# Copies of h and its maxima issued by SyncE instead of GpSimd, and two of the four products of the ones moved behind a later transform

## The chip, the cores and the metric

The kernel runs on one core of a Trainium2 chip. The time is that of the device, in microseconds, from a run of the whole program. Before the change it is 1114.31 us, the median of 3 runs (1113.95 to 1114.52). One further execution was profiled; its own time is 1113.99 us, and the span of the trace is 1112.2 us.

## The reference

```python
# x: (8, 3136, 256)
X = np.fft.fft(x, axis=1)
X = np.fft.fft(X, axis=2)
x = X.real.reshape(25088, 256)          # 8 * 3136 tokens
h = x @ w_in                            # (25088, 1024)
e = np.exp(h - h.max(-1))
sm = e / (e.sum(-1) + 1e-09)
solu = h * sm
mu, var = mean(solu), mean((solu - mu) ** 2)
ln = (solu - mu) / np.sqrt(var + 1e-06) * g_ln
out = ln @ w_out                        # (25088, 256)
```

A two-dimensional Fourier transform whose real part goes, token by token, through a first weight, a softmax-weighted linear unit, a layer norm, and a second weight. All of it is float32.

## The kernel before, in words

**Units.** The transform over 3136 positions is split as 49 x 64. The kernel treats the eight sequences as four pairs, and for each pair it goes over 24 frequencies k1 of the 49; a unit is one pair at one frequency. Since the input is real, a frequency and its mirror give the same even part and opposite odd parts, so each unit has 128 rows of even part and odd part and two "signs", s = 0 and s = 1, of h: the sum and the difference of the two. That makes 96 units, and two more are put in at places 90 and 91 (`order_of`): the units of frequency zero, each holding the 32 columns of four sequences (`t.m` is 0 or 1 for these two and None for all others). 98 units in all, and 49 batches of two.

**Steps.** After an opening, a loop over i goes through the units. In step i the program works on several of them at once, each engine's instructions in program order (the order is written out by hand and the tiles' dependencies supply the semaphores):

- unit i: `even` (line 318, VectorE), `up` (line 305, TensorE, the first weight), `join` for both signs (lines 334 and 338, VectorE: h and, by the same instruction, its negated maximum), `expo` for both signs (line 346, ScalarE), `product` for both signs (line 353, VectorE), `square` for both signs (line 360, ScalarE), and `turn_both` (line 425, VectorE).
- unit i + 2: `second_transform` (line 269, TensorE), whose result q is taken by ScalarE (`take2`, line 275); then `spread` (line 280), a small copy issued by SyncE.
- unit i - 5: `Down`, the second weight by seven block products instead of eight: p1, p4, p5, p6, p2, p3, p7 (line 502, TensorE, each eight matmuls in the trace). p5, p6, p3 and p7 use sums of blocks, S. X, onto which p6 accumulates, is seeded by a copy of ScalarE (`seed`, line 528) of what p1 made. In ScalarE's queue that copy stands behind the squares of unit i - 1 and the take of q.
- unit i - 4: `sums` (line 495, four additions on GpSimd) make its S. The first of them is made to wait for VectorE's last product of unit i - 1.
- the batch of units i - 2 and i - 1, when i is even: `move_blocks` (line 462), 16 DMAs issued by SyncE, the rest of the transposition.
- unit i - 6: `store`. The rows of sign 0 of a batch go out by four DMAs of SyncE (line 600) when its second unit is done; those of sign 1 by an indirect DMA of GpSimd (line 589).

**SyncE's order in a step.** Stores of unit i - 6 (odd i only, once the batches are shared), spread of unit i + 2, and further down, for even i, the moves. A DMA's waits are made by the engine that issues it, at its place in that engine's program.

**Frequency 1568.** One frequency of the 3136, half of them, comes out of no unit's rows by itself. Its eight rows of h, one for each sequence, are computed apart (`Half`), over the steps before unit 90: `half.h` holds the rows and `half.row` the negated maxima. In steps 90 and 91 (the units of frequency zero) four of them each are put into rows 0, 32, 64 and 96 of sign 1 of h, and their maxima into `nmax`. `give` (lines 876 to 879) does that, after the unit's join and before its exponentials, by two DMAs of GpSimd: line 878 copies the four rows of 1024 numbers, line 879 the four maxima. For these two units the join makes s = 1 first (line 334, then the negation, line 322), then s = 0 (line 338). The second exponential needs both copies.

In GpSimd's queue, step i has: mirror sums (not in steps 90 and 91), `sums`, `give`, `power` (line 415), `store` of sign 1.

**The opening.** The weights come as float64 and are narrowed on the chip. The second weight Wo is narrowed in four pieces of two chunks (`narrow_out`, line 677, VectorE, with ScalarE making the exponents by lines 651 to 655). Its mean over the 1024 rows, wbar, is later subtracted from it (`centre`). The mean's sum is made by TensorE as products with a matrix of ones (`mean_out`, line 782), in two parts: first the four chunks 0 to 3 of Wo, in the opening, ahead of the transforms of units 0 and 1 (line 269); then, in step 1, two chunks that GpSimd's `fold_out` has made of chunks 4 to 7. `keep_mean` (line 786, ScalarE) takes the result. `begin(1)`, near the end of step 0, holds `up` of unit 1 and the transform of unit 3. In step 1 `turn_whole` (line 443) transposes unit 0 on TensorE, ahead of the second part of the mean.

Of the kernel before, what the change touches and what calls it, by code (L numbers as in the profile page):

```python
# [17 lines left out]
P = 128  # L18
# [5 lines left out]
NH = N2 // 2  # L24
# [31 lines left out]
def kernel(  # L56
# [19 lines left out]
    nc = tc.nc  # L76
    B, S, D = x.shape
    FF = moe_w_in.shape[1]
    KF = FF // P
# [26 lines left out]
    Wo = const.tile([P, KF, D], FP32, name="Wo")  # L106
    Ws = const.tile([P, 4, KF // 2, P], FP32, name="Ws")
    ones_ident = const.tile([P, 2 * P], FP32, name="ones_ident")
    ones, ident = ones_ident[:, 0:P], ones_ident[:, P:]
# [11 lines left out]
    def result(i):  # L121

        return banks[i % 4]
# [168 lines left out]
    def column(t):  # L292

        ps = result(3)[:, 0:1]
        nc.tensor.matmul(ps, t.q[0:1, P : 2 * P], ones[0:1, 0:1], start=True, stop=True)
        t.r = small.tile([P, 1], FP32, tag="r", name="r")
        nc.vector.tensor_copy(out=t.r, in_=ps)

    def up(t, c):

        ps = ps_h.tile([P, FF], FP32, tag=f"h{c}", name=f"ps_h{c}")
        whole_even = c == 0 and t.at in MIDDLE
        for half in range(2):
            fs = slice(half * HW, (half + 1) * HW)
            nc.tensor.matmul(ps[:, fs], t.q[:, c * P : (c + 1) * P], Wi[:, c, fs], start=True, stop=not whole_even)  # L305
        if whole_even:
            for half in range(2):
                fs = slice(half * HW, (half + 1) * HW)
                nc.tensor.matmul(ps[:, fs], t.q[0:1, P : 2 * P], w_mid[0:1, fs], start=False, stop=True)
        return ps  # L310

    def even(t, ps):

        t.ev = fpool.tile([P, FF], FP32, tag="ev", name="ev", bufs=1)
        if t.at in MIDDLE:
            nc.scalar.copy(t.ev, ps)
            return
        nc.vector.scalar_tensor_tensor(out=t.ev, in0=w_mid, scalar=t.r, in1=ps,  # L318
                                       op0=ALU.mult, op1=ALU.add)
# [8 lines left out]
    def join(t, s):  # L328

        if t.nmax is None:  # L330
            t.nmax = small.tile([P, 2], FP32, tag="nmax", name="nmax")
        t.h[s] = fpool.tile([P, FF], FP32, tag="h", name="h", bufs=2)
        if s and t.m is not None:
            nc.vector.tensor_tensor_reduce(out=t.h[s], in0=t.ev, in1=t.odd, scale=0.5, scalar=-3.0e38,
                                           op0=ALU.subtract, op1=ALU.max, accum_out=t.nmax[:, s : s + 1])
            negate(t.nmax[:, s : s + 1])
            return
        nc.vector.tensor_tensor_reduce(out=t.h[s], in0=t.h[0] if s else t.ev, in1=t.odd, scale=1.0 if s else -0.5,  # L338
                                       scalar=3.0e38, op0=ALU.add, op1=ALU.min, accum_out=t.nmax[:, s : s + 1])
# [16 lines left out]
    def square(t, s):  # L356

        if s == 0:
            t.ssq = small.tile([P, 2], FP32, tag="ssq", name="ssq")
        nc.scalar.activation(out=t.h[s], in_=t.u[s], func=ACT.Square, bias=t.usum[:, s : s + 1], scale=-float(FF),  # L360
                             accum_out=t.ssq[:, s : s + 1])
# [70 lines left out]
    def turn_whole(t, late=False):  # L432

        uT = t.batch.uT[:, t.w].rearrange("p c i (n s) -> p c (i n) s", s=2)
        n = KF // 2
        t.wait = []
        for s in t.signs:
            for half in range(2):
                bank = (1, 2, 0, 1)[2 * s + half] if late else 2 * s + half + 1
                ps = result(bank).rearrange("p (c k) -> p c k", c=n)  # L440
                for c in range(n):
                    f = half * n + c
                    nc.tensor.matmul(ps[:, c, :], t.u[s][:, f * P : (f + 1) * P], ident, is_transpose=True,
                                     start=(c == 0), stop=(c == n - 1), skip_group_check=True)
                if s or late and half:
                    t.wait.insert(0 if bank == 0 else len(t.wait), (uT[:, half * n : (half + 1) * n, :, s], ps))
                else:
                    nc.scalar.copy(uT[:, half * n : (half + 1) * n, :, s], ps)
# [231 lines left out]
    class Weights:  # L680
# [91 lines left out]
            n = KF // 4 * D  # L772
            nc.gpsimd.tensor_tensor(out=self.part, in0=w[:, 0:n], in1=w[:, n:], op=ALU.add)

        def mean_out(self, half):
            if half == 0:
                self.cs = result(3)[:, 0:D]
                parts = [Wo[:, c, :] for c in range(KF // 2)]
            else:
                parts = [self.part[:, c * D : (c + 1) * D] for c in range(KF // 4)]  # L780
            for c, i in enumerate(parts):
                nc.tensor.matmul(self.cs, ones, i, start=half == 0 and c == 0, stop=half == 1 and c == KF // 4 - 1,
                                 skip_group_check=True)

        def keep_mean(self):
# [56 lines left out]
    class Half:  # L842
# [32 lines left out]

        def give(self, t):
            of = slice(4 * t.m, 4 * t.m + 4)
            nc.gpsimd.dma_start(out=t.h[1][0 : P : NH], in_=self.h[of])
            nc.gpsimd.dma_start(out=t.nmax[0 : P : NH, 1:2], in_=self.row[of, 1:2])

    with tc.manual_schedule():
        pairs = [Pair(p) for p in range(NP)]
        first, weights = pairs[0], Weights()
# [107 lines left out]
        def second_transform(i):  # L991
            if i < len(units):
                t = units[i]
                if t.m is None:
                    take2(t, transform2(pairs[t.p], t.k))
                else:
                    t.q = q_self[t.m]
                if i not in (2, 3) + MIDDLE:
                    spread(t)

        def enter(i):
            cur = units[i]
            if i % 2 == 0:
                batches.append(Batch(i // 2))
            cur.batch, cur.w = batches[-1], i % 2

        def begin(i):

            cur = units[i]
            enter(i)  # L1010
            ps = up(cur, 0)
            if i in (2, 3):
                cur.odd = up(cur, 1)
                column(cur)
            even(cur, ps)
            if i not in (2, 3):
                cur.odd = up(cur, 1)
            second_transform(i + 2)
# [8 lines left out]
        for i in range(whole + 1):  # L1027
            cur = units[i]
            prv = units[i - 1] if i else None
            if prv:  # L1030
                turn_whole(prv, i == 1)
                if i == 1:
                    square(prv, 1)
            if i == 1:
                weights.mean_out(1)
            for s in cur.signs:
                join(cur, s)
            if i == 0:
                weights.narrow_out(3, (2,))
                weights.fold_out()  # L1040
            if 1 < i < whole:
                for o, ps in prv.wait:
                    nc.vector.tensor_copy(out=o, in_=ps)
            for s in cur.signs:
                expo(cur, s)
            if i == 1:
                weights.keep_mean()
            if i in (1, whole):
                for o, ps in prv.wait:
                    nc.scalar.copy(o, ps)  # L1050
            if i == 0:
                begin(1)
            done = units[0 if i == 2 else i - 1 : i] if i > 1 else []
            for t in done:
                stats(t)
            if i == whole:
                nxt = units[i + 1]
                enter(i + 1)
                even(nxt, up(nxt, 0))
            if i == whole:  # L1060
                other_pairs(i, ahead, "fold")
            for s in cur.signs:
                product(cur, s)
                if i < whole and s == 0:
                    square(cur, s)
            if i == 1:
                weights.centre(cur)
            if i == 2:
                weight_sums(cur)
            if i < whole:  # L1070

                if i:
                    begin(i + 1)
                if i:
                    square(cur, 1)
            else:
                for s in cur.signs:
                    square(cur, s)
                other_pairs(i, ahead, "mirror", cur)
                sums(units[1], None, part=slice(2, 4))  # L1080
                turn_both(cur)
                stats(cur)
            for work in ("mirror", "fold", "load") if i < whole else ("load",):
                other_pairs(i, ahead, work, cur)
            if i == whole - 1:
                sums(units[1], None, part=slice(0, 2))
            for t in done:
                power(t)
# [9 lines left out]
        for i in range(whole + 1, len(units) + lag + 1):  # L1098
# [30 lines left out]
            if cur:  # L1129
# [3 lines left out]
                if i == SELF_STEPS[-1]:  # L1133
                    half = Half()
# [165 lines left out]
```

## Time and profile before

| | |
|---|---|
| median of 3 runs | 1114.31 us |
| lowest, highest | 1113.95, 1114.52 us |
| the profiled execution's own time | 1113.99 us |
| its span | 1112.2 us |
| TensorE matmul busy | 1094.5 us, 98% of the span |
| TensorE weight load | 876.8 us, 79% |
| VectorE | 971.2 us, 87% |
| ScalarE | 801.3 us, 72% |
| GpSimd | 786.6 us, 71% |

How to read it: PE is TensorE, PEld its weight loads (which overlap with it), DVE is VectorE, ACT is ScalarE, POOL is GpSimd, SPq is the queue of SyncE. In a timeline each row has the start in us from the span's start, the time it took, engine, source line, operation, what is written and read, shape, and the count of instructions merged into the row; in brackets stands how long the engine had been idle before it and what ended the wait. A wait for several semaphores is put down to one releaser, which need not be the one that mattered. In a list of waits the columns are the total in us, the count, and the longest. In a table of windows the columns are the stretch, its length, the busy time of each engine, the granted clock of TensorE as a share, the share of the DMA engines that was busy, and GB/s.

### The profile page before, as it was taken

The numbers are of one execution on the slowest core, as the hardware profiler recorded it, in microseconds if no ns is written. First come the engines' busy times: TensorE is split into PE (matmuls) and PEld (weight loads), VectorE is DVE, ScalarE is ACT, GpSimd is POOL, SyncE is SP. The second block draws the span as 40 slices with busy tenths as digits, with TensorE's granted clock in tenths as the row PEclk, the third lists the DMA queues.
The fourth block names the chain that finished last, engine by engine and source line by source line (L and its number), as shares of the span: only waits on it lengthen the run. The fifth ranks groups of instructions, "written<-read, shape, count | busy, mean of one in ns | idle before, by whom it ended". The sixth has DMA issues, their size and how long they took to land. (4 is left out here: it accounts for less than half of the span.)

```text
span 1112.2 us, 21997 instructions
## 1 busy us (share of the span) xinstructions
PE 1094.5 (98%) x7083; PEld 876.8 (79%) x7083; DVE 971.2 (87%) x1439; ACT 801.3 (72%) x1964; POOL 786.6 (71%) x661
## 2 busy tenths in 40 slices
PE   8899999999999999999999999999999999999998
PEld 5557878787887878788788787878878877777888
DVE  7998888889898898989989898888898898897984
ACT  5697777777777777777777777777777777676772
POOL 4066888775888878767778887856766766667665
PEclk9999999999999999999999999999999999999999
DMA  9654899878989989868989999976977878766775
GB/s 330 223 178 97 182 183 202 182 141 164 189 148 198 190 188 197 169 130 151 193 154 199 185 190 201 178 142 118 184 143 136 150 142 152 131 122 112 144 134 127
DMA packets 447594, 185.69 MB, mean 167 GB/s; under 512 B 415102, under 2 KB 429454, under 8 KB 447480
## 3 DMA queue, kind: packets, MB, share of 16 engines
q1 hardware_dynamic: 434760, 144.58, 68.5%
q0 software_dynamic: 12720, 39.69, 12.1%
q8 instruction: 58, 0.95, 0.3%
q14 instruction: 56, 0.46, 0.1%
HBM read 46.75 MB, written 38.80 MB: 77 GB/s over the span
## 5 line engine op out<-in xcount | busy, mean ns | idle before, releaser
L305 PE MATMUL ps_h<-Wi,q 128*128 128x512 f32 x768 | 346.7, 593 | 2.0 <-DVE nmax L338 1.7
L495 POOL TENSOR_TENSOR S<-uT 128x512 f32<-128x512 f32 x188 | 239.7, 1275 | 116.4 <-DVE u L353 50.6
L502 PE MATMUL ps_m<-Ws,S 128*128 128x128 f32 x2328 | 301.0, 275 | 2.5 <-POOL S L495 2.5
L502 PEld LDWEIGHTS ps_m<-Ws,S 128*128 128x128 f32 x2328 | 283.3, 192 | 7.8 <-POOL S L495 4.5
L360 ACT ACTIVATE h<-u,usum 128x1024 f32<-128x1024 f32 x196 | 225.0, 1148 | 68.6 <-DVE u L353 68.6
L305 PEld LDWEIGHTS ps_h<-Wi,q 128*128 128x128 f32 x768 | 138.4, 190 | 141.6 <-issue 136.6
L353 DVE SCALAR_TENSOR_TENSOR u<-h,u 128x1024 f32<-128x1024 f32 x196 | 233.7, 1228 | 15.9 <-ACT u L346 15.8
L346 ACT ACTIVATE u<-h,nmax 128x1024 f32<-128x1024 f32 x196 | 223.5, 1142 | 8.1 <-DMA nmax<-half 3.7
L425 DVE STREAM_TRANSPOSE v<-u 128x2048 f32<-128x2048 f32 x92 | 212.6, 2311 | 3.2
L502 PE MATMUL ps_m<-Wo,uT 128*128 128x128 f32 x1552 | 205.5, 275 | 0.0
L502 PEld LDWEIGHTS ps_m<-Wo,uT 128*128 128x128 f32 x1552 | 189.7, 192 | 2.0 <-issue 1.9
L338 DVE CUSTOM_DVE_ANT_0 h<-ev,ps_h 128x1024 f32<-128x1024 f32 x98 | 119.7, 1221 | 17.1 <-DVE ev L318 7.9
L338 DVE CUSTOM_DVE_ANT_0 h<-h,ps_h 128x1024 f32<-128x1024 f32 x96 | 117.2, 1221 | 14.0 <-ACT h L360 0.4
L589 POOL DMA_INDIRECT out_dram<-ot,idx x98 | 108.8, 1110 | 26.9 <-issue 11.5
L495 POOL TENSOR_TENSOR S<-S,uT 128x512 f32<-128x512 f32 x94 | 119.7, 1274 | 7.4
L495 POOL TENSOR_TENSOR S<-uT,S 128x512 f32<-128x512 f32 x94 | 119.8, 1275 | 7.3
L318 DVE SCALAR_TENSOR_TENSOR ev<-w_mid,r,ps_h 128x1024 f32<-128x1024 f32 x97 | 120.3, 1240 | 0.1
L502 PE MATMUL ps_m<-Ws,uT 128*128 128x128 f32 x776 | 102.7, 275 | 0.0
L502 PE MATMUL ps_m<-Wo,S 128*128 128x128 f32 x776 | 102.5, 275 | 0.0
L167 POOL TENSOR_TENSOR xa<-xa,xb 98x510 f32<-98x510 f32 (+1 forms) x48 | 59.3, 1236 | 56.8 <-DVE u L353 45.8
L537 ACT ACTIVATE ot<-ps_m,rs 128x256 f32<-128x256 f32 x97 | 45.9, 473 | 69.5 <-PE ps_m L502 50.3
L502 PEld LDWEIGHTS ps_m<-Ws,uT 128*128 128x128 f32 x776 | 94.7, 192 | 0.0
(141 smaller groups left out, 1191.7 us busy)
## 6 DMA issues: line engine op xcount, KB each, us to landing
uT<-v SPq DMA_DIRECT2D x736, 128.0 KB
out_dram<-ot SPq DMA_DIRECT2D x184, 64.0 KB
g<-zd POOLq DMA_DIRECT2D x18, 640.0 KB, 7.5
zd<-z SPq DMA_DIRECT2D x24, 400.0 KB
xa<-in_x_dram SPq DMA_DIRECT2D x24, 392.0 KB
raw_in<-in_moe_w_in_dram SPq DMA_DIRECT2D x4, 512.0 KB
xa<-in_x_dram SPq DMA_DIRECT2D x4, 512.0 KB
room<-in_x_dram SPq DMA_DIRECT2D x4, 512.0 KB
```

Of the source, the lines that this page charges most:

```text
L167: i = engine.tensor_tensor(out=a[:, :, 1:D], in0=a[:, :, 1:D], in1=rb[:, :, D - 1 : 0 : -1], op=ALU.add)
L305: nc.tensor.matmul(ps[:, fs], t.q[:, c * P : (c + 1) * P], Wi[:, c, fs], start=True, stop=not whole_even)
L318: nc.vector.scalar_tensor_tensor(out=t.ev, in0=w_mid, scalar=t.r, in1=ps, op0=ALU.mult, op1=ALU.add)
L338: nc.vector.tensor_tensor_reduce(out=t.h[s], in0=t.h[0] if s else t.ev, in1=t.odd, scale=1.0 if s else -0.5, scalar=3.0e38, op0=ALU.add, o ...
L346: nc.scalar.activation(out=t.u[s], in_=t.h[s], func=ACT.Exp, bias=t.nmax[:, s : s + 1], scale=sign_of(t, s), accum_out=t.esum[:, s : s + 1])
L353: t.last = nc.vector.scalar_tensor_tensor(out=t.u[s], in0=t.h[s], scalar=sign_of(t, s), in1=t.u[s], op0=ALU.mult, op1=ALU.mult, accum_out= ...
L360: nc.scalar.activation(out=t.h[s], in_=t.u[s], func=ACT.Square, bias=t.usum[:, s : s + 1], scale=-float(FF), accum_out=t.ssq[:, s : s + 1])
L425: nc.vector.transpose(out=v, in_=u)
L495: i = engine.tensor_tensor(out=S[j], in0=a, in1=b, op=op)
L502: nc.tensor.matmul(o, a[:, c], b[:, c], start=start and c == 0, stop=c == n - 1, skip_group_check=True)
L537: nc.scalar.mul(out=self.t.ot[1], in_=self.PP, mul=self.rs[1])
L589: dma = nc.gpsimd.indirect_dma_start(out=out, out_offset=bass.IndirectOffsetOnAxis(ap=idx[:, i : i + 1], axis=0), in_=t.ot[s], in_offset=None)
```

## The change

`give` issues its two DMAs from SyncE. `mean_out` has three parts instead of two: chunks 0 and 1 of Wo stay where the first part was; chunks 2 and 3 follow `begin(1)` at the end of step 0, behind the transform of unit 3; the two folded chunks stay in step 1.

```diff
-        def mean_out(self, half):
-            if half == 0:
+        def mean_out(self, part):
+            n = KF // 4
+            if part == 0:
                 self.cs = result(3)[:, 0:D]
-                parts = [Wo[:, c, :] for c in range(KF // 2)]
-            else:
-                parts = [self.part[:, c * D : (c + 1) * D] for c in range(KF // 4)]
-            for c, i in enumerate(parts):
-                nc.tensor.matmul(self.cs, ones, i, start=half == 0 and c == 0, stop=half == 1 and c == KF // 4 - 1,
+            for c in range(n):
+                i = self.part[:, c * D : (c + 1) * D] if part == 2 else Wo[:, part * n + c, :]
+                nc.tensor.matmul(self.cs, ones, i, start=part == 0 and c == 0, stop=part == 2 and c == n - 1,
                                  skip_group_check=True)
...
         def give(self, t):
             of = slice(4 * t.m, 4 * t.m + 4)
-            nc.gpsimd.dma_start(out=t.h[1][0 : P : NH], in_=self.h[of])
-            nc.gpsimd.dma_start(out=t.nmax[0 : P : NH, 1:2], in_=self.row[of, 1:2])
+            nc.sync.dma_start(out=t.h[1][0 : P : NH], in_=self.h[of])
+            nc.sync.dma_start(out=t.nmax[0 : P : NH, 1:2], in_=self.row[of, 1:2])
...
             if i == 1:
-                weights.mean_out(1)
+                weights.mean_out(2)
...
             if i == 0:
                 begin(1)
+                weights.mean_out(1)
```

## The prediction

> **What bounds the kernel now.** I read the page first, then the list of waits for TensorE, then the timelines of the five engines and SyncE's queue around units 90 and 91 (985 to 1036 us), where the copies stand, and around 40 to 62 us, where the products stand.
>
> ```profile
> PE 1094.5 (98%) x7083; PEld 876.8 (79%) x7083; DVE 971.2 (87%) x1439; ACT 801.3 (72%) x1964; POOL 786.6 (71%) x661
> ```
>
> TensorE is busy for 1094.5 of the span of 1112.2 us: a microsecond by which it stands still in mid-kernel is a microsecond of the end, and one in which it already waits can be filled for nothing. (The page's chain of waits breaks off a few microseconds before the end and carries nothing here.) Its longest wait in total, over the whole kernel, is this:
>
> ```profile
> PE ps_m L502 <- POOL S L495: 2.5, 2, 1.5
> ```
>
> Two waits, 2.5 us. The timeline of TensorE places them at 1011 and 1022, both ahead of a product with S:
>
> ```profile
> 1008.50 1.06 PE L502 MATMUL ps_m<-Ws,S 128*128 128x128 f32 x8
> 1011.02 1.13 PE L502 MATMUL ps_m<-Ws,S 128*128 128x128 f32 x8 [1.46 <-POOL S L495]
> ...
> 1022.41 1.13 PE L502 MATMUL ps_m<-Ws,S 128*128 128x128 f32 x8 [1.02 <-POOL S L495]
> ```
>
> The eight matmuls at 1008.50 are p5, those at 1011.02 are p6. The view names GpSimd's sums as the releaser, but p6 also adds onto X, and X is seeded by ScalarE's copy (line 528). ScalarE's timeline:
>
> ```profile
> 1006.71 1.15 ACT L346 ACTIVATE u<-h,nmax 128x1024 f32<-128x1024 f32 x1 [2.37 <-DMA nmax<-half]
> ...
> 1010.65 0.27 ACT L528 COPY ps_m<-ps_m 128x128 f32<-128x128 f32 x1
> ...
> 1018.10 1.15 ACT L346 ACTIVATE u<-h,nmax 128x1024 f32<-128x1024 f32 x1 [1.37 <-DMA nmax<-half]
> ```
>
> The seed ends at 1010.92, and p6 starts 0.1 us later. The seed stands in ScalarE's queue behind the second square, which needs VectorE's second product, which needs the second exponential, and that one waited 2.37 us for the copied maximum of unit 90. From the exponential's start to p6 it is 1011.02 - 1006.71 = 4.31 us; for unit 91 it is 1022.41 - 1018.10 = 4.31 us again. So the two stalls of TensorE, 1.46 and 1.02 us, are the late landings of these copies, and **the start of p6 follows the landing of the maximum of unit 91 by a fixed 4.31 us**. After it TensorE is dense again, so what that landing shifts, the end shifts.
>
> **The copies, before.** When is their source ready, and when are they issued? VectorE's timeline, then GpSimd's:
>
> ```profile
> 1001.65 0.08 DVE L334 DVE_READ_ACCUMULATOR2_ANT nmax<- 128x1 f32 x1
> 1001.77 0.15 DVE L322 TENSOR_SCALAR nmax<-nmax 128x1 f32<-128x1 f32 x1
> ...
> 1014.16 0.15 DVE L322 TENSOR_SCALAR nmax<-nmax 128x1 f32<-128x1 f32 x1
> ```
>
> ```profile
> 1002.12 0.67 POOL L878 DMA_DIRECT2D h<-half  x1
> 1002.80 0.59 POOL L879 DMA_DIRECT2D nmax<-half  x1
> ...
> 1015.14 0.56 POOL L879 DMA_DIRECT2D nmax<-half  x1
> ```
>
> The rows they overwrite are ready at 1001.73 and 1001.92 (unit 90); the maximum of unit 91 at 1014.31. GpSimd comes to them within a microsecond, straight after its four sums. From issue to landing the maximum takes (its line's view):
>
> ```profile
> DMA to landing us min/median/max: 2.9/3.4/3.9
> ```
>
> The longer one is unit 90's (1002.80 + 3.9 = 1006.70), the shorter unit 91's. What the change takes off GpSimd, 2 x (0.65 + 0.57) us, is worth nothing: at 71% busy it is nobody's bound, and its next sums are ordered behind a product of VectorE that itself hangs on the copied maximum.
>
> **The copies, after.** SyncE's queue runs in program order. Here is what stands in it, by its timeline, and then the time of one issue of each kind, by the lines' views (ns, shortest/median/longest):
>
> ```profile
> 981.46 13.44 SPq L462 DMA_DIRECT2D uT<-v  x16
> ...
> 1001.29 13.35 SPq L462 DMA_DIRECT2D uT<-v  x16
> 1014.75 2.67 SPq L600 DMA_DIRECT2D out_dram<-ot  x4
> 1017.52 5.18 SPq L280 DMA_DIRECT2D r<-q  x2
> ```
>
> ```profile
> L280 SPq DMA_DIRECT2D r<-q x3: 533/533/542, 998.4 to 1022.2; - x3
> L462 SPq DMA_DIRECT2D uT<-v x48: 627/706/1428, 981.5 to 1036.6; - x48
> L600 SPq DMA_DIRECT2D out_dram<-ot x12: 422/531/1157, 995.0 to 1040.0; - x12
> ```
>
> In step 90 the order is: spread of unit 92 (done by 999), the two copies, then the 16 moves of units 88 and 89. In step 91: four stores, the spread of unit 93 (the first of the two at 1017.52, so done at 1018.06), the two copies. Two consequences follow.
>
> Unit 90. SyncE is free, and waits at the copies until 1001.73. With the spread's 0.54 us for each issue h goes at about 1001.8 and the maximum at 1002.35. That is a new wait, and what is queued behind it are the 16 moves: they begin at about 1003.0 rather than 1001.29, **1.7 us late**. Nobody needs the moved blocks soon (sums of unit 88 come two steps on, after 1020), but the queue does. For a landing of a transfer issued by SyncE the trace has one clean case, early on, where the next issue in the same queue waits for it:
>
> ```profile
> 41.33 0.27 SPq L250 DMA_DIRECT2D zd<-z_g  x1
> 43.27 0.38 SPq L257 DMA_DIRECT2D g<-zd  x1
> ```
>
> ```profile
> SPq L257 <- DMA zd<-z_g: 0.3, 1, 0.3
> ```
>
> That is 1.94 us from issue to landing; I take it, since at 1002 SyncE has nothing outstanding. The maximum lands at 1004.3, about when the first exponential ends (2.37 us before 1006.71, thus 1004.34). The stall of 1.46 us goes.
>
> Unit 91. The maximum is ready by 1014.3 at the latest, but SyncE is then still issuing the moves. Without any delay it would come to the copies at 1018.06; with the 1.7 us of unit 90's wait, at 1019.8, with 0.1 between groups 1019.9. h takes 0.54, so the maximum is issued at 1020.4 and lands, at 1.94 us, at 1022.4. Before, the exponential began at 1018.10. It begins **4.3 us later**, and p6 with it: 1026.7 instead of 1022.4. The 1.46 us gained a step before are swallowed, because they only let TensorE wait longer at this p6 (some 6.8 us rather than 1.02). Everything behind this p6 (the square, the sums, the moves of units 90 and 91) hangs on the same landing and shifts along. This term is +4.3 us.
>
> Its bounds. Cheaper: issues at the 0.42 us of the shortest store, which makes the delay 1.3 and the copy of h shorter by 0.1, and stores that as a group take 0.7 us less: +3.0. Dearer: h waits until the join's second half is through (about 1003.0, 1.3 us more), or the landing takes GpSimd's shortest 2.9 us (+1.0), or GpSimd's issue times (+0.3): up to about +7.0 together. A gain is excluded by the queue: even with no delay at all the maximum of unit 91 is issued no earlier than 1018.06 + 0.54 and lands at 1020.5, which is +2.4. I stay at 1.94 because the stores' data will have nearly run out when the copies are issued.
>
> The Trainium skill (DMA: Bandwidth & Descriptors, Latency and other measured facts) puts the first byte of a transfer from SyncE's path at about 600 ns and of one from GpSimd's at about 1 µs. Taken off the 2.9 us of the row above, that would be a landing of 2.5 us, an estimate from that page, and the sum would be +4.9; the 1.94 us of the trace stand nearer.
>
> **The products of the ones.** Two chunks, four matmuls, leave the place before the first transform and go behind the transform of unit 3. What they held up and what they meet, TensorE, then ScalarE, then TensorE again:
>
> ```profile
> 46.19 1.13 PE L782 MATMUL ps_m<-Wo,ones_ident 128*128 128x256 f32 x4 [1.20 <-DVE Wo L677]
> ```
>
> ```profile
> 46.61 0.72 ACT L651 ACTIVATE S<-S,limits 128x512 f32<-128x512 int32 x1
> 47.37 0.73 ACT L653 ACTIVATE S<-S,limits 128x512 f32<-128x512 f32 x1
> 48.00 0.35 ACT L275 COPY q<-ps_m 128x256 f32<-128x256 f32 x1
> ```
>
> ```profile
> 56.67 0.61 PE L269 MATMUL ps_m<-T,g 128*128 128x128 f32 x4
> 58.03 2.46 PE L443 MATMUL ps_m<-ones_ident,u 128*128 128x128 f32 x16 [0.76 <-DVE u L353]
> 60.33 1.03 PE L782 MATMUL ps_m<-Ws,ones_ident 128*128 128x256 f32 x4
> ```
>
> Before the transform they cost a wait of 1.20 us and up to 1.03 us of work. But the result of the transform is taken by ScalarE at 48.00, back to back behind its own work, and the first product with the first weight waits for that. An earlier transform is taken no earlier: gain 0. In the new place four matmuls need at most 1.03 us from about 57.2; TensorE stands idle there for 0.76 us until 58.03, so at most 0.3 us of delay reaches the transposes, and these wait in part for ScalarE anyway. I take 0. With that cover gone it would cost the full 1.03; a gain has no path, since ScalarE decides.
>
> **The sum.** Against the profiled execution's own 1113.99 us (span 1112.2): +4.3 + 0 = 1118.3. It lies 0.3 under the median of the runs, 1114.31; on that median the forecast is 1118.6, range of this case 1117.3 to 1121.3. What a measurement here can tell from no change is about 0.2%, or 2.2 us.
>
> **Rivals.** *Both stalls vanish, faster.* If the 16 moves are issued faster than I assume, SyncE reaches the copies of unit 91 in time. The point that decides: h must be issued by about 1018.10 - 1.94 - 0.54 = 1015.6, so that moves, stores and spread together take 12.6 us from 1003.0, and even then the second stall only stays as it is; to be rid of it takes another microsecond. For it: the shortest issue of a move is 0.627, and 16 of those are 10.0 us. Against it: each group of 16 took 13.4, and the DMA engines were full meanwhile:
>
> ```profile
> 1010.00:1015.00 5.00, 3.98 (x33) 3.87 (x34) 4.79 (x6) 2.71 (x10) 4.84 (x5) 1.00 0.99 165
> ```
>
> (share 0.99, next to last column). It would give 1114.31 - 2.5 = 1111.8. Chance 0.08.
>
> *Who issues does not matter.* The copies land for both units when they did before, as if only 1.2 us of issue time passed from one queue to another whose owner has room for it: 1114.3. It needs the copies of unit 91 to get past the moves and stores ahead of them. The Trainium skill says something near to this (DMA: Bandwidth & Descriptors, Issuing engines are not separate DMA queues): whichever engine starts a transfer, it runs on the same 16 DMA engines, and the choice saves only the issuer's usually small time. By that rule this would be the outcome. What speaks against is SyncE's queue, in which 16.8 us of issues (1001.29 to 1018.06) stand ahead. Chance 0.08.
>
> *Later still.* The small copies land behind the stores' data, or the late moves hold up the sums of unit 88: above 1121.3. Chance 0.04.
>
> **Numbers.** The forecast has 0.80, and its own range is the range given. Faster 0.08, same 0.08, slower 0.84.
>
> **What would show it.** In SyncE's timeline the copies of unit 90 at about 1001.8 and 1002.4, the moves at 1003.0; the copies of unit 91 near 1019.9 and 1020.4. ScalarE's wait for the maximum of unit 90 gone, that of unit 91 grown from 1.37 to some 8 us; one p6 with about 6.8 us of idle time, the other with none. In the beginning, q still taken at 48.0. I am wrong if the copies of unit 91 are issued before 1018, or if the time does not rise by 2.2 us.

## The result, and the profile after

| | before | after |
|---|---|---|
| median of 5 runs | 1114.31 us | 1120.36 us |
| lowest, highest | 1112.51, 1114.52 us | 1118.69, 1120.69 us |
| the profiled execution's own time | 1113.99 us | 1120.36 us |
| its span | 1112.2 us | 1118.6 us |

The kernel before has two more runs here than above, with the same median. The changed kernel is slower by 6.05 us; the ratio is 1.0055, with an interval of 1.004 to 1.007. The forecast was 1118.6 us, its range 1117.3 to 1121.3.

SyncE's timeline after, from the copies of unit 90 to those of unit 91 (start, duration, instruction):

```profile
1001.25 0.59 SPq L877 DMA_DIRECT2D h<-half  x1
1001.94 0.56 SPq L878 DMA_DIRECT2D nmax<-half  x1
1002.60 13.88 SPq L462 DMA_DIRECT2D uT<-v  x16
1016.59 2.43 SPq L600 DMA_DIRECT2D out_dram<-ot  x4
1019.11 0.55 SPq L280 DMA_DIRECT2D r<-q  x1
1019.76 0.59 SPq L877 DMA_DIRECT2D h<-half  x1
1020.45 0.53 SPq L878 DMA_DIRECT2D nmax<-half  x1
```

The copies of unit 90 go out as soon as their rows are free. Then the queue holds 16 moves, four stores and a spread, and only behind them, at 1020.45, comes the maximum of unit 91, which GpSimd had issued at 1015.14. What that does to ScalarE, in its timeline after (second exponentials of units 90 and 91, then the seed of X):

```profile
1003.72 1.13 ACT L346 ACTIVATE u<-h,nmax 128x1024 f32<-128x1024 f32 x1
...
1022.22 1.15 ACT L346 ACTIVATE u<-h,nmax 128x1024 f32<-128x1024 f32 x1 [8.48 <-DMA nmax<-half]
...
1026.16 0.27 ACT L528 COPY ps_m<-ps_m 128x128 f32<-128x128 f32 x1
```

Unit 90's exponential waits for nothing any more (2.37 us before); unit 91's waits 8.48 us instead of 1.37. TensorE's timeline after, at the p6 that hangs on it:

```profile
1018.11 1.06 PE L502 MATMUL ps_m<-Ws,S 128*128 128x128 f32 x8
1026.53 2.04 PE L502 MATMUL ps_m<-Ws,S 128*128 128x128 f32 x8 [7.36 <-POOL S L495]
1028.36 1.92 PE L502 MATMUL ps_m<-Wo,uT 128*128 128x128 f32 x8
1030.07 1.91 PE L502 MATMUL ps_m<-Wo,S 128*128 128x128 f32 x8
1031.78 1.14 PE L502 MATMUL ps_m<-Ws,S 128*128 128x128 f32 x8
1032.75 3.60 PE L305 MATMUL ps_h<-Wi,q 128*128 128x512 f32 x8
```

One wait of 7.36 us has replaced the two of 1.46 and 1.02. From the exponential's start to p6 it is 1026.53 - 1022.22 = 4.31 us, as before. But look at the durations behind the wait: p6, p2 and p3 take 1.8 us each from start to start, where the same rows before took 0.9. From p6 to the first product of `up` it is 1032.75 - 1026.53 = 6.22 us; in the trace before:

```profile
1023.38 1.06 PE L502 MATMUL ps_m<-Wo,uT 128*128 128x128 f32 x8
1024.27 1.06 PE L502 MATMUL ps_m<-Wo,S 128*128 128x128 f32 x8
1025.16 1.06 PE L502 MATMUL ps_m<-Ws,S 128*128 128x128 f32 x8
1026.06 3.60 PE L305 MATMUL ps_h<-Wi,q 128*128 128x512 f32 x8
```

There it was 1026.06 - 1022.41 = 3.65. The busy time by windows of the trace after says what happened (window, length, busy time of the five engines; the granted TensorE clock is third from the end):

```profile
1016.00:1019.00 3.00, 3.00 (x29) 2.98 (x27) 0.00 (x0) 0.00 (x0) 0.00 (x0) 1.00 0.89 167
1022.00:1026.00 4.00, 0.00 (x0) 0.00 (x0) 2.47 (x3) 3.61 (x7) 1.13 (x1) 0.50 0.00 0
1026.00:1031.00 5.00, 4.47 (x21) 4.50 (x22) 4.68 (x6) 2.50 (x12) 3.91 (x4) 0.50 0.01 0
1032.00:1035.00 3.00, 3.00 (x14) 1.80 (x14) 2.40 (x5) 2.38 (x5) 1.74 (x2) 1.00 0.97 158
```

The granted clock falls to 0.50 during the wait and stays there for some 5 us of work behind it. So the 6.4 us between the two spans are p6's start, 1026.53 against 1022.41, +4.12; the stretch behind it at half the clock, 6.22 against 3.65, +2.57; and the rest up to the end, 1118.6 - 1032.75 against 1112.2 - 1026.06, -0.29.

### The profile page after: what moved, and what is told of

The parts are those of the page before. It is cut to its first block, busy times and chain, and to the rows that moved or that the text cites. A ratio compares the mean times of both kernels' runs of the same rounds, so it can differ in the third digit from the quotient of the medians.

```text
span 1118.6 us, 21992 instructions
## 1 busy us (share of the span) xinstructions
PE 1095.4 (98%) x7083; PEld 878.5 (79%) x7083; DVE 973.5 (87%) x1439; ACT 801.0 (72%) x1964; POOL 785.0 (70%) x657
## 4 chain that ended last, share of the span: by engine, by line
PE 87%; DVE 5%; DMA 2%; SPq 2%; issue 1%; POOL 1%; ACT 1%; POOLq 0%; DVEq 0%; ACTq 0%
PE ps_m L502 51%; PE ps_h L305 27%; PE ps_m L242 4%; PE ps_m L269 4%; SPq L462 1%; POOL S L495 1%; DMA xa<-in_x_dram 1%; DVE h L338 1%; DVE u L353 1%; DVE ev L318 1%; PE ps_m L572 1%; DVE S L627 1%; DVE S L671 0%; DVE xa L167 0%; DMA raw_in<-in_moe_w_in_dram 0%
## 5 line engine op out<-in xcount | busy, mean ns | idle before, releaser
L269 PEld LDWEIGHTS ps_m<-T,g 128*128 128x128 f32 x400 | 59.7, 191 | 46.4 <-issue 43.1
L502 PEld LDWEIGHTS ps_m<-Wo,S 128*128 128x128 f32 x776 | 95.3, 193 | 0.0
```

Of the source, the lines that this page charges most:

```text
L269: nc.tensor.matmul(o, g[:, k, h * P : (h + 1) * P], table, start=(h == 0), stop=True, skip_group_check=True)
L502: nc.tensor.matmul(o, a[:, c], b[:, c], start=start and c == 0, stop=c == n - 1, skip_group_check=True)
```

## The experiments

The theory under test: the copies of unit 91, behind the moves, stores and spread in SyncE's queue, cost about 4.3 us through the landing, and the half clock behind the long wait about 2.5 more; the moved products cost nothing. The rivals: that the products have a share, that unit 90's copies (the new wait ahead of the moves) are what costs, and that the clock is an accompaniment rather than a cost. All ratios are to the kernel before, run on the same chip.

**Each part alone.** The kernel before with the two DMAs of `give` on SyncE:

```
-            nc.gpsimd.dma_start(out=t.h[1][0 : P : NH], in_=self.h[of])
-            nc.gpsimd.dma_start(out=t.nmax[0 : P : NH, 1:2], in_=self.row[of, 1:2])
+            nc.sync.dma_start(out=t.h[1][0 : P : NH], in_=self.h[of])
+            nc.sync.dma_start(out=t.nmax[0 : P : NH, 1:2], in_=self.row[of, 1:2])
```

> The copies from SyncE for both units, the products left where they were. Theory (queue and clock): everything the change costs is here, the copies of unit 91 behind the 16 moves, the stores and a spread (p6 later by 4 to 4.6 us), and TensorE at half its granted clock for some 5 us after a wait of over 7 us (2.6 us more): 1120.3, the profile with one p6 that waits 7.0 to 7.6 us and a granted clock of 0.50 right after it. Rival (products): one to two microseconds of the 6.05 are due to the products in their new place, so 1118.3 to 1119.3 here.

1119.92 against 1113.22 us, ratio 1.0056 (1.0043 to 1.0069): within these intervals the copies are the whole loss. Its TensorE timeline shows the same wait and the same slow stretch, 1032.45 - 1026.01 = 6.44 us:

```profile
1026.01 2.05 PE L502 MATMUL ps_m<-Ws,S 128*128 128x128 f32 x8 [6.97 <-POOL S L495]
...
1032.45 1.88 PE L305 MATMUL ps_h<-Wi,q 128*128 128x512 f32 x4
```

The other part, the changed kernel with those two lines put back on GpSimd, so that only the products are moved:

> The products moved, the copies left with GpSimd. Theory (ScalarE takes q no earlier, and TensorE stands idle in the new place): 1114.3, within 0.5 of the kernel before; q taken at the same distance from the product with the first weight, the transposes of unit 0 begin no later than 0.3 us behind the end of VectorE's product. Rival (products): 1115.3 to 1116.3. Second rival (the wait taken away in the opening is a gain): 1113.1.

1114.35 against 1113.22, ratio 1.0008 (0.9999 to 1.0017). Here nothing could be told by the time alone, and the span, 1114.1, is 1.9 us over that of before; so the same kernel was run again:

> The kernel with the products moved and nothing else, once more on another chip: the first time it measured 0.08% over the kernel before, with the interval touching zero, while its trace showed no change at the edit. Theory (nothing at the edit, the rest chance of the moves' landings at 300 and 570 us): within 0.05% of the kernel before. Rival (a cost of about a microsecond that the opening's trace doesn't show): 0.08% or more over it again, the interval clear of zero.

1112.84 against 1113.37, ratio 0.9999 (0.999 to 1.0008). The two agree with zero. What the first span had more did not arise at the products: it came around 300 and 570 us, as the last section tells.

**One unit alone.** Unit 90's copies on SyncE, unit 91's left on GpSimd, in the kernel before:

```
+            engine = nc.sync if t.m == 0 else nc.gpsimd
+            engine.dma_start(out=t.h[1][0 : P : NH], in_=self.h[of])
+            engine.dma_start(out=t.nmax[0 : P : NH, 1:2], in_=self.row[of, 1:2])
```

> Unit 90's copies from SyncE, unit 91's from GpSimd, products as before. Theory (the queue ahead decides): unit 90's stall of 1.46 us by the wait, 1.7 us by the spacing of the products, goes; the moves begin 1.7 us late and nobody feels it; unit 91 keeps its wait of about 1 us: 1112.7. Rival (the late moves cost): the sums of unit 88 or p1 come late, 1114.3 or more.

1111.59 against 1113.22, ratio 0.9986 (0.9978 to 0.9995): faster, by 1.63 us. TensorE's timeline:

```profile
1008.08 1.95 PE L502 MATMUL ps_m<-Ws,S 128*128 128x128 f32 x16
...
1019.97 1.13 PE L502 MATMUL ps_m<-Ws,S 128*128 128x128 f32 x8 [0.70 <-POOL S L495]
```

p5 and p6 of the first step stand as one group of 16: the stall of 1.46 us is gone, and the second is 0.70 instead of 1.02. SyncE's new wait ahead of the moves (they begin at 1002.69) costs nothing by itself; that rival is out. (How long the first stall is when GpSimd issues the copies differs from trace to trace; see the last section.) The reverse, unit 91 alone on SyncE, has the two engines swapped in that first line:

> Unit 90's copies from GpSimd, unit 91's from SyncE, products as before. Theory (queue): the moves are on time, SyncE comes to the copies at 1018.1, the maximum lands at 1020.5, p6 goes 2.4 us later than before with a wait of about 3.5 us. 1116.7 if TensorE keeps its clock over such a wait, 1119.3 if it falls to half as after the 7.4 us wait. Rival (who issues does not matter): 1114.3.

1119.33 against 1113.22, ratio 1.0045 (1.0032 to 1.0059). TensorE's timeline:

```profile
1025.88 2.05 PE L502 MATMUL ps_m<-Ws,S 128*128 128x128 f32 x8 [5.53 <-POOL S L495]
...
1031.40 1.88 PE L305 MATMUL ps_h<-Wi,q 128*128 128x512 f32 x4
```

A wait of 5.53 us, and 1031.40 - 1025.88 = 5.52 us behind it where 3.65 are due: 1.9 us of loss by the clock. Unit 91 alone makes the loss. The 1119.3 us expected came out, but partly by luck: p6 starts 3.47 us later than before instead of 2.4, and the clock takes 1.9 instead of 2.6. One of its six runs took 1115.95 us at a mean granted clock of 0.998, the other five 1119.20 to 1119.68; of that run there is no trace, and the difference of 3.4 us is more than the 1.9 us of the clock.

**Is the half clock a cost?** To take it away without touching the wait, the wait has to be filled. Into the changed kernel went 14 further products, which are no part of the computation, into the unused half of a result that nobody reads, ahead of p6 of step 92:

```
+                if i == 92:
+                    for _ in range(14):
+                        nc.tensor.matmul(result(3)[:, NW // 2 :], ident, T[0].rearrange("p b k n -> p (b k n)")[:, 0 : NW // 2], start=False, stop=True, skip_group_check=True)
                 new.p6()
```

> The changed kernel with 14 extra products of the identity with a table, 6.1 us of TensorE's time, set between p5 and p6 of step 92 into columns of the bank that nobody reads: they lie inside the wait of about 7 us. Theory (idleness takes the clock away): p6 starts as late as in the changed kernel, but the granted clock stays 1.00, p6, p2 and p3 take 0.9 us each rather than 1.7 to 1.8, and the time is 2.5 us under the changed kernel's, 1117.4. Rival (the products behind the wait are slow for another reason, such as the moves or the traffic): 1120, no change.

1126.71 against 1113.7, ratio 1.0119 (1.0104 to 1.0134). It did not do what it was meant to. TensorE's timeline:

```profile
1029.08 8.86 PE L1141 MATMUL ps_m<-T,ones_ident 128*128 128x256 f32 x28 [7.15 <-ACT ps_m L528]
1037.78 1.05 PE L502 MATMUL ps_m<-Ws,S 128*128 128x128 f32 x8
```

The result they write to is the one that X and its seed (line 528) belong to, so they waited for the seed themselves and ran behind the wait, not in it. They took the slow stretch upon them, and p6 behind them, at 1.05, runs at full clock again. The second try puts the same 14 products into another result, `result(1)`, between p5 and `keep_p`:

```
                 new.p5()
+                if i == 92:
+                    for _ in range(14):
+                        nc.tensor.matmul(result(1)[:, NW // 2 :], ident, T[0].rearrange("p b k n -> p (b k n)")[:, 0 : NW // 2], start=False, stop=True, skip_group_check=True)
                 new.keep_p()
```

> The changed kernel with 14 extra products of the identity with a table (6.1 us at full clock), set straight behind p5 of step 92 into columns of p5's own bank that nobody reads, so that they wait for nothing that is late; the earlier try had put them into the bank of the seed, and they began only when the wait was over. Theory (idleness takes the clock away): they fill the wait, p6 starts as late as in the changed kernel, the granted clock stays 1.00, p6 to p7 take 3.6 us rather than 6.2, and the time is 2.5 us under the changed kernel's: 1117.4. Rival (the products behind the wait are slow for another reason): no change, 1120.

1117.42 against 1113.15, ratio 1.004 (1.0026 to 1.0053). TensorE's timeline, then its windows:

```profile
1019.44 6.21 PE L1128 MATMUL ps_m<-T,ones_ident 128*128 128x256 f32 x28
1026.13 1.13 PE L502 MATMUL ps_m<-Ws,S 128*128 128x128 f32 x8 [0.48 <-POOL S L495]
...
1029.78 3.60 PE L305 MATMUL ps_h<-Wi,q 128*128 128x512 f32 x8
```

```profile
1022.00:1026.00 4.00, 3.65 (x17) 2.86 (x16) 2.87 (x3) 3.83 (x9) 1.45 (x2) 1.00 0.00 0
1026.00:1031.00 5.00, 4.87 (x35) 4.25 (x36) 4.68 (x8) 4.18 (x15) 4.72 (x5) 1.00 0.28 42
```

The extra products occupy TensorE for 6.21 us (the same 28 rows took 8.86 in the failed try, 2.65 more, at the lower clock), the clock stays at 1.00, and from p6 to `up` it is 1029.78 - 1026.13 = 3.65 us, as before the change. The loss of 2.57 us is gone although p6 starts no sooner than its landing allows. This span is 1115.6, 3.0 us below that of the changed kernel; the medians' ratios, 1.0055 and 1.004, differ by 1.7 us and their intervals overlap, so the size rests on the trace.

**Longer.** Both copies on SyncE, and `give` placed behind `move_blocks`, so that unit 90's also stand behind 16 moves:

```
-            if cur and cur.m is not None:
-                half.give(cur)
...
                 move_blocks(batches[i // 2 - 1], slice(0, 2))
+            if cur and cur.m is not None:
+                half.give(cur)
```

> The kernel before with the copies issued by SyncE, but in step 90 behind the 16 moves and not ahead of them. Theory (what stands ahead in SyncE's queue decides): the maximum of unit 90 is issued after 1014.6 and lands near 1017, p6 of step 91 waits some 12 us and TensorE loses its clock there; unit 91's copies then find SyncE free, and its wait goes: 1113.2 + 10.5 + 2.6 - 1.2 = 1125.1. Rival (the copies pass the moves since the DMA engines take all queues in turn): within 2 us of the changed kernel, 1118 to 1122.

1126.2 against 1113.7, ratio 1.0113 (1.0098 to 1.0129). SyncE's timeline, then TensorE's:

```profile
1001.65 13.47 SPq L462 DMA_DIRECT2D uT<-v  x16
1015.22 0.62 SPq L878 DMA_DIRECT2D h<-half  x1
1015.94 0.68 SPq L879 DMA_DIRECT2D nmax<-half  x1
```

```profile
1022.40 2.05 PE L502 MATMUL ps_m<-Ws,S 128*128 128x128 f32 x8 [12.48 <-POOL S L495]
...
1028.58 1.88 PE L305 MATMUL ps_h<-Wi,q 128*128 128x512 f32 x4
```

Place in the queue is the price: the moves go first, the maximum leaves at 1015.94 and TensorE waits 12.48 us. The slow stretch is 1028.58 - 1022.40 = 6.18 us, no longer than behind 7.36 us of waiting.

**A third queue.** The kernel before with both copies on ScalarE (`nc.scalar.dma_start`):

> The kernel before with the copies issued by ScalarE for both units. Theory (the queue ahead decides): ScalarE has nothing of the sort ahead of them; unit 90's maximum lands near 1005.5 as its moves have begun by then, unit 91's in time; of the stalls of 1.69 and 1.26 us some 0.5 us is left, minus what ScalarE spends on issuing: 1110.8, 2.4 under the kernel before. Rival (ScalarE's issue time, 4 x 0.6 us, takes the place of the wait): 1113 or more.

1116.56 against 1113.7, ratio 1.0035 (1.0023 to 1.0048): slower, where a gain was expected. The expectation was wrong. SyncE's timeline of that run, then the waits of its queue:

```profile
981.71 26.23 SPq L462 DMA_DIRECT2D uT<-v  x16
```

```profile
SPq L462 <- DMA h<-half: 13.4, 1, 13.4
```

The moves of step 88, 13.2 to 13.5 us in all other traces, take 26.23, because one of them waits 13.4 us for ScalarE's copy of h, which the program issues two steps later. In the list of the built program's instructions the DMAs of SyncE and ScalarE take their completion semaphores (the counters by which a transfer reports that it has landed) from one set of eight in turn, and a DMA waits until the one that had its semaphore before it has landed; two places among the moves had gone to ScalarE's copies. In that list it is the twelfth of the 16 moves that waits for the copy of h, and in the trace the last five are issued together from 1004.24 on. No run tested the reading by itself, and how the 13.4 us become 2.9 us of the median was not followed. With unit 90 on SyncE and only unit 91 on ScalarE (`nc.sync if t.m == 0 else nc.scalar`) the exposure is small:

> The kernel before with unit 90's copies from SyncE (free then, ahead of the moves) and unit 91's from ScalarE (idle then). Theory: both stalls go, 1.69 + about 1.2: 1110.3, 2.9 under the kernel before and a little under the one with unit 90 alone from SyncE. Rival (the second stall stays as its landing is slow beside the moves from any queue): 1111.6, as with unit 90 alone.

1111.42 against 1113.7, ratio 0.9984 (0.9975 to 0.9993). In TensorE's timeline neither p6 waits, both stand in one group with their p5; SyncE's moves take 15.46 us, 2 more than usual, without a wait of TensorE. The median is 2.3 us under the kernel before, not the 2.9 expected, and little different from that with unit 90 alone (0.9986):

```profile
1008.21 1.95 PE L502 MATMUL ps_m<-Ws,S 128*128 128x128 f32 x16
...
1018.34 1.95 PE L502 MATMUL ps_m<-Ws,S 128*128 128x128 f32 x16
```

**The changed kernel, mended.** Last, only unit 91's copies were taken off SyncE in the changed kernel, first to GpSimd, then to ScalarE:

> The changed kernel, products moved as well, with unit 91's copies back on GpSimd's queue and unit 90's left on SyncE's. Theory (only what stands ahead of unit 91's copies costs, the products cost nothing): as with unit 90's copies alone, 1111.6, some 2 us under the kernel before, one wait at p6 of about 0.7 us and no loss of clock. Rival (the products cost what their run alone seemed to show, 0.9 us): 1112.5.

1112.5 against 1113.15, ratio 0.9996 (0.9987 to 1.0005). The median is the one the rival expected, a cost of the products, and not the 1111.6 of the theory; but the run above with the products alone, at 0.9999, speaks against that cost, and the interval here does not decide. In its trace the p6 behind unit 90's copies has no wait and the one behind unit 91's 0.31 us, and the span is 1110.0.

> The changed kernel with unit 91's copies issued by ScalarE, unit 90's left with SyncE, products moved. Theory: no wait at either p6, as with the products left in place, 0.16% to 0.25% under the kernel before. Rival (the products cost a microsecond): 0.1% under it at most.

1112.06 against 1113.37, ratio 0.9987 (0.9976 to 0.9997), between theory (0.16% or more) and rival (0.1% at most); no wait at either p6. All four versions with unit 90 on SyncE and unit 91 elsewhere are ahead of the changed kernel. Three of them are ahead of the kernel before too, by 0.13 to 0.16%; the fourth (products moved, unit 91 on GpSimd) can't be told from it. A cost of the moved products of up to 0.1% is not excluded by these runs.

## Why the prediction was right, and what it missed

**SyncE's queue: right.** Every place came out within 0.6 us of what was worked out. The copies of unit 90 are issued at 1001.25 and 1001.94 (predicted 1001.8 and 1002.35), the moves at 1002.60 (1003.0), the maximum of unit 91 at 1020.45 (1020.4). The profile after runs 0.52 us early at this point: `up` of step 90 starts at 992.18 instead of 992.70. (It is 0.93 us early at line 242 already, ahead of both edits, as the rows further below show.) Counted from there, the moves are 1.83 us late (1.7), they take 13.88 us (13.35), and the maximum leaves 28.27 us after that `up` (27.70). Its landing takes 1022.22 - 1020.45 = 1.77 us, under the 1.94 taken from the opening and well under the 2.5 us estimated from the Trainium skill. Together the term is 4.12 + 0.52 = 4.64 us where the sum had 4.3.

**Unit 90's stall goes, and is swallowed: right.** The list of TensorE's waits after has one where there were two:

```profile
PE ps_m L502 <- POOL S L495: 7.4, 1, 7.4
```

The one wait is 7.36 us (predicted 6.8), ScalarE's 8.48 (8). That p6 follows the second exponential, and with it the landing, by 4.31 us held, to 0.01, wherever p6 waited for it: 1022.22 to 1026.53 after, 1021.57 to 1025.88 with unit 91 alone, 1018.09 to 1022.40 behind the moves, and before; with both copies on ScalarE, where VectorE's product took 0.3 us longer, it was 4.61. The distance alone doesn't say who releases p6, because the next sums of GpSimd hang on the same product. But the sums that p6 reads are made a step earlier, and in the trace after the one it needs ended at 1009.01; the seed ended at 1026.43, 0.10 us ahead of p6. So it is the seed, and not the sums that the view names.

**The step that failed** is one sentence: "After it TensorE is dense again, so what that landing shifts, the end shifts." TensorE is dense there, but at half its clock: +2.57 us, which the sum has not got and no bound named. 4.64 + 2.57, less 0.29 at the end and 0.52 that the profile was early, are the 6.4 us between the spans. The measured time lies within the range only because its upper end was set by other costs (a late h, a slow landing), none of which occurred: that is luck. At this place the trace before could not show the fall, since its longest wait there was 1.46 us, with no loss behind it. But it shows it in the opening, ahead of the stretch from 40 us on that the prediction read. TensorE's timeline before, then its windows:

```profile
10.95 5.37 PE L731 MATMUL wps<-w_in,Q 128*128 128x512 f32 x8 [2.30 <-DMA Q<-in_q_tab_dram]
...
40.52 3.60 PE L731 MATMUL wps<-w_in,w_mid 128*128 128x512 f32 x8
```

```profile
12.00:14.00 2.00, 2.00 (x3) 0.67 (x2) 1.69 (x4) 1.07 (x2) 1.39 (x3) 0.50 1.01 329
```

Behind a wait of 2.30 us the clock is at 0.50, and eight products take 5.37 us that take 3.60 later: 1.8 us lost. A charge for a longer wait could have been put into the sum from these rows.

The Trainium skill (TensorE: Matmul & The Clock Gate, HAM oscillation — how this bites in real kernels) gives the rule that was not weighed: no idle gap of TensorE over about 3.4 us, or it is put back to half rate; the table of its Part 1: The HAM clock gate adds that about 3.4 us of sustained work bring the full rate back. The runs agree in part: nothing was lost behind 1.46 us, and the clock was at 0.50 behind 7.36 us; but the 2.30 us of the opening, under that bound, were enough too. An estimate by that page of the Trainium skill would be 3.4 us at half rate, 1.7 lost; 2.57 was measured.

**The products: right at zero, and for the reason given.** Counted from the start of the block of first transforms (line 242, 24 matmuls), `up` of unit 2 comes 24.76 us later in the trace before and 24.74 after:

```profile
36.44 4.25 PE L242 MATMUL ps_m<-y,F 98*100 98x258 f32 x24 [1.83 <-DVE y L182]
...
61.20 1.02 PE L305 MATMUL ps_h<-Wi,q 128*128 128x512 f32 x2
```

```profile
35.51 4.25 PE L242 MATMUL ps_m<-y,F 98*100 98x258 f32 x24 [1.87 <-DVE y L182]
...
46.06 1.16 PE L269 MATMUL ps_m<-T,g 128*128 128x128 f32 x8 [1.99 <-DMA g<-zd]
...
56.17 1.03 PE L781 MATMUL ps_m<-Wo,ones_ident 128*128 128x256 f32 x4
57.09 2.46 PE L443 MATMUL ps_m<-ones_ident,u 128*128 128x128 f32 x16
60.25 2.31 PE L305 MATMUL ps_h<-Wi,q 128*128 128x512 f32 x5
```

q is taken at 47.06, which is 11.55 us from that block against 48.00 - 36.44 = 11.56 before: ScalarE decides, as argued. In this trace the transform starts only 0.16 us sooner on that scale (10.55 against 10.71), because it waits 1.99 us for g. The first run of the products alone shows it better. TensorE, then ScalarE:

```profile
36.47 4.25 PE L242 MATMUL ps_m<-y,F 98*100 98x258 f32 x24 [1.50 <-DVE y L182]
...
46.10 1.16 PE L269 MATMUL ps_m<-T,g 128*128 128x128 f32 x8 [1.07 <-DMA g<-zd]
```

```profile
48.03 0.35 ACT L275 COPY q<-ps_m 128x256 f32<-128x256 f32 x1
```

There the transform starts 1.08 us sooner (9.63 us from the block), and q is still taken at 11.56. In the new place, in the trace after, the four products fill the 0.76 us in which TensorE stood idle, and the transposes start behind them without a gap, 21.58 us from the block (21.59 before).

**The rivals.** Both stalls vanishing needed moves issued faster than in 12.6 us with stores and spread; they took 1019.66 - 1002.60 = 17.1. That who issues does not matter is refuted: a place behind 16 moves in the issuing queue cost 6 us. The rule of the Trainium skill that stood beside it (DMA: Bandwidth & Descriptors, Issuing engines are not separate DMA queues) is right that the issue time itself matters little (0.56 to 0.67 us for each copy on GpSimd before, 0.53 to 0.59 on SyncE after), but does not count the place in the queue.

## What to carry to other kernels

A DMA on an issuing engine is priced by what stands ahead of it in that engine's program order, not by its own issue time: two copies of half a microsecond did well with the queue free (unit 90) and cost 6 us behind 17 us of other issues (unit 91). A long wait of TensorE is charged twice, once for the wait and once for the slow clock behind it (1.9 to 2.8 us here, behind waits of 5.5 us and more), and filling it with work that waits for nothing took the second charge away. And a gain ahead of a later wait on the same chain is no gain: look for the last one.

## What the runs showed beyond that

**The clock after a wait.** The length of TensorE's wait and what the stretch from p6 to `up` took beyond 3.65 us: 1.46 before, no loss; 2.12 with the copies on ScalarE, no loss; 5.53, 1.9 us; 6.97, 2.8; 7.36, 2.57; 12.48, 2.53. At this place the loss doesn't grow with the wait once it is there. The length of one wait is not all that counts, though: 2.30 us in the opening lost 1.8 us, and in the repetition of the products alone 24 products at line 242 took 5.81 us behind a wait of 1.65 us, at a clock of 0.50 from 38 to 40 us, while before they took 4.25 behind 1.83. What else decides is open.

**Shared completion semaphores** of SyncE and ScalarE: 13.4 us of waiting for a DMA that the program issues later, told above.

**A landing that varies.** GpSimd's copy of unit 90's maximum lands 3.91 us after its issue in the trace before and 2.07 after it (1003.47 to 1005.54) with only unit 91's copies moved to SyncE, where the stall of unit 90 is gone too. It is not the edit: with the products alone moved it took 3.91 us in one trace and 2.73 in the other (1003.90 to 1006.63), with stalls of 1.46 and 0.28 us; that is one kernel, run on two chips. So the 1.46 us that SyncE takes away at unit 90 are what two traces show, not a fixed price of GpSimd; why the landing varies is open.

**Time that wanders in mid-kernel.** Around 300 and 570 us the traces differ by 0 to 1.8 us, at places that no edit touches: GpSimd's sums wait for the landing of the moves for different lengths. One such wait between 290 and 330 us is 2.6 us before and 6.6 with the products alone.

Differences of one or two tenths of a per cent between medians are therefore read here only together with the trace at the place of the edit.
